# Reordering the first batch's attention front and the u additions of a fused attention and mixer kernel

## The chip, the cores and the metric

The kernel runs on one core of a Trainium2 chip. The metric is the device time of one execution in microseconds. The engines are TensorE (PE, with its weight loads as PEld), VectorE (DVE), ScalarE (ACT), GpSimd (POOL) and SyncE (SP), each with its own queue of instructions that it takes in order; they wait for each other and for transfers through semaphores.

## The reference

Two layers follow each other: a linear attention with a cosine weighting, and a mixer that works first over the tokens and then over the channels.

```
q, k, v: (8, 8, 576, 64) float32     # batch, head, token, head dim
phi(x) = [relu(x) * cos(theta), relu(x) * sin(theta)]      # 128 features, theta = pi/2 * pos / 576
kv  = einsum('bhsf,bhsd->bhfd', phi(k), v);   z = sum over s of phi(k)
x   = einsum('bhsf,bhfd->bhsd', phi(q), kv) / (einsum('bhsf,bhf->bhs', phi(q), z) + 1e-6)
x   = x as (8, 576, 512)
h   = relu(x^T @ w_tok1) @ w_tok2       # w_tok1 576 x 256, w_tok2 256 x 576
u   = x + h^T
out = u + relu(u @ w_ch1) @ w_ch2       # w_ch1 512 x 1536, w_ch2 1536 x 512
```

## The kernel before

The 576 tokens of a batch are four chunks of 128 (ci 0 to 3, R = 4 in the code) and a tail of 64 (ci = R); the tails of two batches share one tile of 128 rows, the even batch in its lower half and the odd batch in its upper half. The chunks' attention outputs are made in the order ORDER = (0, 1, 2, R, 3). All matmuls take bf16 and accumulate in float32 in PSUM.

A batch has a front and a channel part. The front, class Front, consists of:

- feature (L246; k_side and q_side call it twice, for cosine and sine): phi(k) and phi(q) from the loaded float32 tiles kt and qt into kp and qp, on DVE (L263), or on ACT (L261) where on_act is set.
- values (L266): the cast of v into v_aug, whose extra column of ones gives sums. With nc.scalar it is on ACT, with nc.vector on DVE, with nc.gpsimd on POOL.
- ksum, ksum_out and dens, dens_out (L278 to L308): only in batch 0. z is summed by one-column matmuls (ks_ps, L285), copied by ACT (ks_sb, L293), and multiplied with the transposed phi(q) by one-column matmuls (d_ps, L301); DVE adds 1e-6 and takes the reciprocal (L307, L308). In the other batches the column of ones gives the denominator inside num.
- kv and kv_out (L310, L329): kv in two halves of four heads (kv_ps), copied to kv_sb, half 0 by ACT and half 1 by DVE.
- q_trans (L336): phi(q) transposed on PE (qT_ps) and copied by ACT to qpT, L345. From the third batch on a DMA transposes instead.
- num (L354): 65-column matmuls into num_ps and DVE's division into x_sb (L370).
- tok1, tok1_out (L374, L386): x times w_tok1 into two banks b_ps (L383), and the relu into B.
- tok2 (L392): B times w_tok2 (u_ps, L407), DVE's addition of x (u_sb, L410), and, except in batch 0, a cast by ACT.

The channel part, class Channel, first makes h1T in 12 column blocks (c steps: four matmuls into c_ps each, L552, and a relu on ACT, L556), then the outputs in o steps (o_ps, L585; the addition of u on DVE, L590; a DMA out).

The schedule is written by hand: the order in the program is each engine's order. The function first_front (L643) writes out batch 0's front. In it, busy(idle_ps, n) issues n matmuls on zeros (L204) whose result nobody reads. At its end batch 0's u is not yet there in rows: its transposed form is made directly in PSUM, as x turned by the identity (turned_x, L423, 16 matmuls of 128 columns) plus B times w_tok2 (turned_b, L431, 8 matmuls of 512 columns), is copied to uT by ACT and DVE (L712), and feeds the first three c steps (c_block, L562).

From then on the front of the next batch is put between the steps of the channel part of the one before. The method pieces (L462) gives a list of (slot, what, arguments); what stands in slot i is issued behind step i. For the second batch (first is true there) the steps are those of batch 0, of which c steps 3 to 11 come first and o steps from O = 12 on. This list also holds batch 0's own u (before.tok2, in the list as u), POOL's casts of v, and POOL's three loads of w_ch2 (load_w_ch2, L194). The loads of the third batch's k and q wait for the second of those (L765).

PSUM has eight banks: ps_mm has four buffers of one bank, ps_at two buffers of two banks. A new tile in a pool waits until the tile that held its buffer has been read.

Of the kernel before, what the change touches and what calls it, by code (L numbers as in the profile page):

```python
# [9 lines left out]
F32 = mybir.dt.float32  # L10
BF16 = mybir.dt.bfloat16
AF = mybir.ActivationFunctionType
# [4 lines left out]
def kernel(  # L17
# [15 lines left out]
    nc = tc.nc  # L33
# [3 lines left out]
    Dm = H * D  # L37
    S_tok, D_tok = moe_w_tok1.shape
    Dm2, D_ch = moe_w_ch1.shape
    P = 128  # L40
    R = S // P
    SM = R * P
    ST = S - SM
    NSC = R + 1
    NCC = Dm // P
    NT = D_tok // P
    NCH = D_ch // P
    HH = H // 2
    D1 = D + 1
    DP = 80  # L50
    DH = Dm // 2
# [3 lines left out]
    ORDER = (0, 1, 2, R, 3)  # L55
# [16 lines left out]
    ps_mm = ctx.enter_context(tc.tile_pool(name="ps_mm", bufs=4, space=bass.MemoryType.PSUM))  # L72
    ps_at = ctx.enter_context(tc.tile_pool(name="ps_at", bufs=2, space=bass.MemoryType.PSUM))
# [128 lines left out]
    def busy(dst, times):  # L202
        for _i in range(times):
            nc.tensor.matmul(dst, ident, zeros[:, 0:dst.shape[-1]], start=True, stop=True)  # L204

    def cast_tok1(mi):
        nc.scalar.copy(w_tok1[:, :, mi * P:(mi + 1) * P], w_tok1n[:, :, mi * P:(mi + 1) * P])
# [8 lines left out]
    class Front:  # L216
# [109 lines left out]
                                     stop=(ci == NSC - 1 and j == HH - 1),  # L326
                                     skip_group_check=True)

        def kv_out(self, halves=(0, 1)):  # L329
            for g in halves:  # L330
                copy = nc.vector.tensor_copy if g else nc.scalar.copy
                copy(self.kv_sb[g][:, :, 0:D1],  # L332
                     self.kv_ps[g][:, 0:HH * DP]
                     .rearrange("p (j d) -> p j d", d=DP)[:, :, 0:D1])

        def q_trans(self, ci, heads=(0, H), eng=nc.scalar, pool=ps_mm):  # L336
            lo, hi = heads
            qT_ps = pool.tile([P, hi - lo, P], BF16, name="qT_ps",
                              tag="mm" if pool is ps_mm else "at")
            for h in range(lo, hi):  # L340
                nc.tensor.transpose(qT_ps[:, h - lo, :],  # L341
                                    self.q_of(ci)[:, h, :, :].rearrange("p a b -> p (a b)"), ident)
            dst = self.qpT[:, ci * H + lo:ci * H + hi, :] if ci < R else self.tail.qpT[:, lo:hi, :]
            if eng is nc.scalar:
                nc.scalar.copy(dst, qT_ps)  # L345
            else:
                nc.vector.tensor_copy(dst, qT_ps)
# [3 lines left out]
            nc.sync.dma_start_transpose(out=dst,  # L351
                                        in_=self.q_of(ci).rearrange("p h a b -> p (h a b)"))

        def num(self, ci, fill=0, dens=False):  # L354
            num_ps = ps_at.tile([P, 2, 512], F32, name="num_ps", tag="at")
            if fill:
                busy(num_ps[:, 0, HH * DP:512], 1)
            for h in range(H):
                g, j = divmod(h, HH)
                nc.tensor.matmul(num_ps[:, g, j * DP:j * DP + D1], self.qT_of(ci, h),  # L360
                                 self.kv_sb[g][:, j, 0:D1], start=True, stop=True)
            rows = self.rows_of(ci)
            nv = num_ps[rows, :, 0:HH * DP].rearrange("p g (j d) -> p g j d", d=DP)
            if dens:
                den = self.d_sb[ci][rows].rearrange("p (g j) o -> p g j o", g=2)
            else:
                den = small.tile([P, 2, HH, 1], F32, name="den")[rows]
                nc.vector.tensor_scalar_add(den, nv[:, :, :, D:D1], 1e-6)  # L368
                nc.vector.reciprocal(den, den)
            nc.vector.tensor_mul(  # L370
                self.x_of(ci)[rows].rearrange("p (g j d) -> p g j d", g=2, j=HH),
                nv[:, :, :, 0:D], den.to_broadcast([rows.stop - rows.start, 2, HH, D]))
# [10 lines left out]
                nc.tensor.matmul(self.b1_ps[mi], w, self.x_of(ci),  # L383
                                 start=(ci == ORDER[0]), stop=(ci == ORDER[-1]))

        def tok1_out(self, mi, on_act=True):  # L386
            if on_act:
                nc.scalar.activation(self.B1[:, mi, :], self.b1_ps[mi], AF.Relu)  # L388
            else:
                nc.vector.tensor_relu(self.B1[:, mi, :], self.b1_ps[mi])  # L390

        def tok2(self, ci, pool=None, turn=True):  # L392
            res, tail = self.res, self.tail
# [26 lines left out]

            self.res["uT"] = keep.tile([P, R * NCC, P], BF16, name="uT")

        def turned_x(self, dst, kb, first):  # L423

            for ci in range(R):
                nc.tensor.matmul(dst[:, ci * P:(ci + 1) * P],
                                 self.x[:, ci, kb * P:(kb + 1) * P], ident, start=first,
                                 stop=False, skip_group_check=True)
                first = False

        def turned_b(self, dst, kb, cols):  # L431

# [29 lines left out]
        def pieces(self, b, before):  # L462
# [7 lines left out]
            if first:  # L470

                u, act, pool = before.tok2, nc.scalar, nc.gpsimd
                plan = [(4, KS, 0), (4, KS, 1), (5, u, 0, ps_at, False), (5, KS, 2, True),
                        (6, KS, 3, True), (6, u, 1, ps_at, False), (7, KS, R), (7, V, R, nc.vector), (8, V, 0, act),
                        (8, V, 2, pool), (8, load_w_ch2, 0), (8, V, 3, pool),
                        (8, load_w_ch2, 1), (8, load_w_ch2, 2),
                        (8, u, 2, None, False), (9, V, 1, act), (9, u, 3, None, False),
                        (9, QS, 0), (10, u, R, None, False)]
                plan += [(11, KV, ci) for ci in range(NSC)]
                plan += [(11, QS, 1), (11, QS, 2), (11, self.kv_out),  # L480
                         (11, QT, 0, (0, H), act, ps_at), (11, QT, 1), (11, QS, R),
                         (O, QT, 2), (O, N, 0), (O, QS, 3), (O + 1, QT, R),
                         (O + 1, N, 1), (O + 3, N, 2), (O + 3, QT, 3),
                         (O + 5, N, R), (O + 7, N, 3), (O + 8, before.tail_cast)]
            else:
                if late:
                    plan = [(C + 5, V, 1, nc.vector), (C + 5, V, 3, nc.vector),
                            (C + 6, V, 0, nc.scalar), (C + 6, V, 2, nc.scalar),
                            (C + 7, V, R, nc.scalar)]
                else:  # L490
                    plan = [(C + at, V, ci, nc.scalar)
                            for ci, at in enumerate((-1, -1, 0, 1, 2))]

                if odd:
                    sides = ((-4, KS, 0), (-3, QS, 0), (0, KS, 1), (0, KS, 2), (1, QS, 1),
                             (1, KS, 3), (1, QS, 2), (2, QS, 3))
                elif late:
                    sides = ((-4, KS, 0), (-3, KS, 1), (0, KS, 2), (1, KS, 3), (1, QS, 0),
                             (2, QS, 1), (3, QS, 2), (4, QS, 3), (5, KS, R), (9, QS, R))
                else:  # L500
                    sides = ((-4, KS, 0), (-3, KS, 1), (0, KS, 2), (1, KS, 3), (1, QS, 0),
                             (2, KS, R), (2, QS, 1), (3, QS, 2), (4, QS, R), (5, QS, 3))
                for at, side, ci in sides:
                    plan.append((C + at, side, ci))
                    if side == QS:
                        plan.append((C + at, self.q_trans_dma, ci))

                plan += [(C + at, KV, ci) for ci, at in
                         enumerate((7, 7, 8, 8, 8) if late else
                                   (2, 3, 4, 5, 6) if odd else (2, 3, 4, 6, 7))]  # L510
                plan.append((C + (8 if late else 6 if odd else 7), self.kv_out))
# [131 lines left out]
    def first_front(f):  # L643
# [21 lines left out]
            busy(idle_ps, 2)  # L665
            f.ksum(ci)
        f.k_side(R)
        busy(idle_ps, 2)
        f.ksum(R)
        f.values(R, nc.vector)  # L670
        for ci in range(R):
            f.values(ci, nc.scalar, lo_heads)
            f.values(ci, nc.vector, hi_heads)
        f.ksum_out()
        for ci in range(NSC):
            f.kv(ci, (0,))
            if ci < R - 1:
                busy(idle_ps, 1)
        f.kv_out((0,))
        for ci in range(NSC):  # L680
            f.kv(ci, (1,))
        f.kv_out((1,))
        for ci in range(NT):
            cast_tok1(ci)
        permute_tok2(0, nc.scalar.copy)
        permute_tok2(1, nc.gpsimd.tensor_copy)
        f.new_uT()
        t_ps = {}

        dens = f.dens(ORDER[:2])  # L690
        f.dens_out(*dens)
        f.num(ORDER[0], dens=True)
        dens = f.dens(ORDER[2:])
        f.num(ORDER[1], dens=True)
        f.dens_out(*dens)
        for i, ci in enumerate(ORDER):
            if i + 2 < NSC:
                f.num(ORDER[i + 2], dens=True)
            for mi in range(NT):
                f.tok1(mi, (ci,))  # L700
        for mi in range(NT):
            f.tok1_out(mi, on_act=(mi == 0))
        for kb in range(NCC):
            t_ps[kb] = (ps_mm.tile([P, SM], F32, name="t_ps", tag="mm") if kb < 2 else
                        ps_at.tile([P, 2, 512], F32, name="t_ps", tag="at")[:, 0, :])
            f.turned_x(t_ps[kb], kb, first=True)

        c = Channel(0, f.res, f.tail)
        by_block = f.res["uT"].rearrange("p (r k) t -> p r k t", r=R)
# [105 lines left out]
```

## Time and the profile before

| what | us |
|---|---|
| median of 3 runs | 269.42 |
| lowest and highest of them | 268.97, 269.98 |
| the profiled execution | 268.4 |
| its span, first to last instruction | 266.6 |
| PE busy in the span | 260.2 |
| DVE, ACT, POOL busy | 166.1, 127.5, 12.3 |
| batch 0's front, to its first c_block matmul | 24.1 |
| first matmul of batch 0's o steps | 39.0 |

The span begins with the first instruction and ends with the last; the profiled execution's time is 1.8 us longer than its span. Starts in the timelines count from the span's start. A group's length in a timeline reaches to the modelled end of its last instruction, so for matmuls and for DVE instructions the distance from start to start, not the length, tells the rate. PEclk, the granted clock, is 1.00 over the whole span.

### The profile page before, as it was taken

How to read it: one execution, taken by the hardware profiler on the slowest of the kernel's cores; microseconds unless marked ns; L12 is line 12 of the kernel's file. 1: busy time of each engine (PE TensorE's matmuls, PEld its weight loads, DVE VectorE, ACT ScalarE, POOL GpSimd, SP SyncE). 2: the span in 40 equal slices, each digit the busy share in tenths (PEclk: the TensorE clock that was granted, in tenths of full speed). 3: DMA queues.
4: the chain of work that ended last, by engine and by line, in shares of the span. 5: the costliest groups of instructions: out<-in, count | busy, mean ns of one | idle time of the engine just before them, and what ended most of it. 6: DMA issues, size and time to landing. Idle time of an engine off the chain costs nothing.

```text
span 266.6 us, 5133 instructions
## 1 busy us (share of the span) xinstructions
PE 260.2 (98%) x2042; PEld 139.9 (52%) x2063; DVE 166.1 (62%) x381; ACT 127.5 (48%) x224; POOL 12.3 (5%) x26
## 2 busy tenths in 40 slices
PE   7999999999999999999999999999999999999995
PEld 3675466465644455446644455446644455445544
DVE  6974699785665946785565846876565846720022
ACT  4953976428515461646515462546516362516500
POOL 6410130000000000000000000000000000000000
DMA  6999999779998999459984989289974580180022
GB/s 218 331 285 270 331 165 239 277 191 300 172 373 247 293 194 340 111 154 267 178 299 121 294 218 350 65 179 241 242 252 118 157 121 0 50 208 2 2 89 107
DMA packets 91959, 53.68 MB, mean 201 GB/s; under 512 B 59424, under 2 KB 87072, under 8 KB 91936
## 3 DMA queue, kind: packets, MB, share of 16 engines
q1 hardware_dynamic: 88576, 49.62, 70.0%
q0 software_dynamic: 2832, 3.21, 7.3%
q10 hardware_dynamic: 528, 0.52, 0.6%
q8 instruction: 16, 0.26, 0.4%
q14 instruction: 7, 0.06, 0.1%
HBM read 35.85 MB, written 9.44 MB: 170 GB/s over the span
## 4 chain that ended last, share of the span: by engine, by line
PE 86%; DVE 9%; DMA 2%; issue 1%; DVEq 0%
PE o_ps L585 34%; PE c_ps L552 25%; PE b_ps L383 6%; PE u_ps L407 6%; PE ct_ps L572 4%; PE kv_ps L321 3%; PE num_ps L360 3%; DVE x_sb L370 3%; DVE qp L263 2%; DMA qt<-in_q_dram 2%; PE idle_ps L204 1%; PE c_ps L562 1%; DVE u_sb L410 1%; PE qT_ps L341 1%; DVE den L368 1%
## 5 line engine op out<-in xcount | busy, mean ns | idle before, releaser
L585 PE MATMUL o_ps<-w_ch,h1T 128*128 128x512 bf16 (+2 forms) x392 | 92.7, 366 | 0.6
L552 PE MATMUL c_ps<-uT,w_ch 128*128 128x512 bf16 (+2 forms) x384 | 91.9, 372 | 0.1
L556 ACT ACTIVATE h1T<-c_ps 128x512 bf16<-128x512 f32 x93 | 55.4, 598 | 60.0 <-PE c_ps L552 59.7
L585 PEld LDWEIGHTS <-h1T 128*128 128x128 bf16 x408 | 37.6, 98 | 39.4
L552 PEld LDWEIGHTS <-w_ch 128*128 128x128 bf16 x384 | 33.6, 97 | 29.8
L590 DVE TENSOR_TENSOR o_sb<-o_ps,u_sb 128x512 f32<-128x512 f32 (+2 forms) x34 | 22.4, 659 | 29.2 <-PE o_ps L585 27.2
L410 DVE TENSOR_TENSOR u_sb<-u_ps,x_sb 128x512 f32<-128x512 f32 x32 | 21.7, 689 | 5.8 <-PE u_ps L407 5.6
L414 ACT CAST u_bf<-u_sb 128x512 bf16<-128x512 f32 x28 | 17.2, 618 | 16.7 <-DVE u_sb L410 16.7
L407 PE MATMUL u_ps<-B,w_tok 128*128 128x512 bf16 x79 | 22.4, 379 | 0.2
L388 ACT ACTIVATE B<-b_ps 128x512 bf16<-128x512 f32 x8 | 4.8, 597 | 34.1 <-PE b_ps L383 34.1
L370 DVE TENSOR_TENSOR x_sb<-num_ps,den 128x512 bf16<-128x512 f32 x28 | 19.4, 691 | 1.0
L572 PEld LDWEIGHTS <-w_ch 128*128 128x128 bf16 x192 | 13.9, 98 | 8.7
L263 DVE TENSOR_SCALAR kp<-kt,cos_t 128x512 bf16<-128x512 f32 x32 | 15.2, 479 | 4.2 <-DMA kt<-in_k_dram 4.2
L383 PE MATMUL b_ps<-x_sb,w_tok 128*128 128x512 bf16 x63 | 17.7, 379 | 0.1
L572 PE MATMUL ct_ps<-uT_tail,w_ch 128*128 128x128 bf16 x192 | 16.9, 219 | 0.0
L263 DVE TENSOR_SCALAR qp<-qt,cos_t 128x512 bf16<-128x512 f32 (+1 forms) x35 | 15.8, 452 | 0.5 <-DMA qt<-in_q_dram 0.5
L263 DVE TENSOR_SCALAR qp<-qt,sin_t 128x512 bf16<-128x512 f32 (+1 forms) x35 | 15.8, 452 | 0.0
L274 ACT CAST v_aug<-vt 128x512 bf16<-128x512 f32 (+1 forms) x28 | 15.5, 584 | 0.1
L590 DVE TENSOR_TENSOR o_sb<-o_ps,u_tail 128x512 f32<-128x512 f32 x4 | 2.8, 692 | 19.0 <-PE o_ps L585 19.0
L332 DVE CAST kv_sb<-kv_ps 128x260 bf16<-128x260 f32 x8 | 3.4, 431 | 17.1 <-ACT kv_sb L332 15.9
L360 PEld LDWEIGHTS <-qpT 128*128 128x128 bf16 x256 | 11.5, 98 | 4.9 <-issue 0.7
L263 DVE TENSOR_SCALAR kp<-kt,sin_t 128x512 bf16<-128x512 f32 x28 | 13.4, 480 | 0.0
(94 smaller groups left out, 232.1 us busy)
## 6 DMA issues: line engine op xcount, KB each, us to landing
out_dram<-o_sb SPq DMA_DIRECT2D x31, 256.0 KB, 3.2
kt<-in_k_dram SPq DMA_DIRECT2D x7, 1024.0 KB, 6.9
vt<-in_v_dram SPq DMA_DIRECT2D x7, 1024.0 KB, 7.6
qt<-in_q_dram SPq DMA_DIRECT2D x7, 1024.0 KB, 9.1
w_ch<-in_moe_w_ch_dram POOLq DMA_DIRECT2D x4, 384.0 KB, 10.7
w_ch<-in_moe_w_ch_dram POOLq DMA_DIRECT2D x3, 512.0 KB, 8.0
out_dram<-o_sb SPq DMA_DIRECT2D x9, 128.0 KB, 2.3
qtt<-in_q_dram SPq DMA_DIRECT2D x8, 128.0 KB, 5.2
```

Of the source, the lines that this page charges most:

```text
L263: nc.vector.tensor_scalar(o_ap, i_ap, scalar1=w, scalar2=0.0, op0=ALU.mult, op1=ALU.max)
L360: nc.tensor.matmul(num_ps[:, g, j * DP:j * DP + D1], self.qT_of(ci, h), self.kv_sb[g][:, j, 0:D1], start=True, stop=True)
L370: nc.vector.tensor_mul(self.x_of(ci)[rows].rearrange("p (g j d) -> p g j d", g=2, j=HH), nv[:, :, :, 0:D], den.to_broadcast([rows.stop - r ...
L383: nc.tensor.matmul(self.b1_ps[mi], w, self.x_of(ci), start=(ci == ORDER[0]), stop=(ci == ORDER[-1]))
L407: nc.tensor.matmul(u_ps, w_tok2[:, ki, ci * P:(ci + 1) * P], self.B1[:, ki, :], start=(ki == 0), stop=(ki == NT - 1))
L410: nc.vector.tensor_add(u, u_ps[rows], self.x_of(ci)[rows])
L414: nc.scalar.copy(self.ub[:, ci, :], u)
L552: nc.tensor.matmul(c_ps[:, lo:hi], w_ch1[:, ki, mi * P:(mi + 1) * P], uT[:, lo // P:hi // P, ki, :], start=(ki == 0), stop=(ki == NCC - 1))
L556: nc.scalar.activation(self.h1T[:, mi, :], c_ps, AF.Relu)
L572: nc.tensor.matmul(self.ct_ps[:, mi % R, :], w_ch1[:, ki, mi * P:(mi + 1) * P], self.tail.uT[:, ki, :], start=(mi % R == 0 and ki == 0), s ...
L585: nc.tensor.matmul(o_ps, h, w_ch2[:, ki, cols], start=ki == 0, stop=ki == NCH - 1)
L590: nc.vector.tensor_add(o_sb, o_ps, u)
```

## The change

It touches only batch 0's front, the list for the second batch, and one copy.

- In first_front, the four heads' first half of kv is begun ahead of the last ksum, DVE's four casts of v are issued ahead of ACT's, and all denominators (both dens groups with their DVE instructions) come ahead of kv's second half. Of the busy matmuls behind the k features one of two goes for the last ksum, and the three between the kv chunks go.
- kv's second half is copied by ACT instead of DVE, between the two casts of w_tok1.
- Two of the four turned_x groups do their first three chunks ahead of the last tok1 pair.
- B's relu is done in two halves of 256 columns on each of ACT and DVE.
- In the second batch's list, batch 0's u(0) to u(3) move to c steps 3 to 6, with PSUM from ps_at, and the first k features to step 6, behind u(3); u(R) moves from step 10 to step 8. The sine of q chunk 2 moves from DVE to ACT.
- The copy of the transposed tail of an odd batch's q, where PE transposes it, takes only that batch's 64 columns.

```
@@ Front.kv_out, q_trans, tok1_out, turned_x
-        def kv_out(self, halves=(0, 1)):
+        def kv_out(self, halves=(0, 1), on_act=(0,)):
             for g in halves:
-                copy = nc.vector.tensor_copy if g else nc.scalar.copy
+                copy = nc.scalar.copy if g in on_act else nc.vector.tensor_copy
...
+            if ci == R and self.rows.start:
+                dst, qT_ps = dst[:, :, self.rows], qT_ps[:, :, self.rows]
...
+        def tok1_out(self, mi, on_act=True, cols=slice(0, Dm)):
...
-        def turned_x(self, dst, kb, first):
-            for ci in range(R):
+        def turned_x(self, dst, kb, chunks=range(R)):
+            for ci in chunks:
@@ Front.pieces, first
-                plan = [(4, KS, 0), (4, KS, 1), (5, u, 0, ps_at, False), (5, KS, 2, True),
-                        (6, KS, 3, True), (6, u, 1, ps_at, False), (7, KS, R), (7, V, R, nc.vector), (8, V, 0, act),
+                plan = [(3, u, 0, ps_at, False), (4, u, 1, ps_at, False), (5, u, 2, ps_at, False),
+                        (6, u, 3, ps_at, False), (6, KS, 0), (6, KS, 1), (6, KS, 2, True),
+                        (7, KS, 3, True), (8, u, R, None, False), (8, KS, R),
+                        (8, V, R, nc.vector), (8, V, 0, act),
                         (8, V, 2, pool), (8, load_w_ch2, 0), (8, V, 3, pool),
-                        (8, load_w_ch2, 1), (8, load_w_ch2, 2),
-                        (8, u, 2, None, False), (9, V, 1, act), (9, u, 3, None, False),
-                        (9, QS, 0), (10, u, R, None, False)]
+                        (8, load_w_ch2, 1), (8, load_w_ch2, 2), (9, V, 1, act), (9, QS, 0)]
                 plan += [(11, KV, ci) for ci in range(NSC)]
-                plan += [(11, QS, 1), (11, QS, 2), (11, self.kv_out),
+                plan += [(11, QS, 1), (11, QS, 2, True), (11, self.kv_out),
@@ first_front
         f.k_side(R)
-        busy(idle_ps, 2)
-        f.ksum(R)
         f.values(R, nc.vector)
         for ci in range(R):
+            f.values(ci, nc.vector, hi_heads)
+        for ci in range(R - 1):
             f.values(ci, nc.scalar, lo_heads)
-            f.values(ci, nc.vector, hi_heads)
+        f.kv(0, (0,))
+        busy(idle_ps, 1)
+        f.ksum(R)
         f.ksum_out()
-        for ci in range(NSC):
-            f.kv(ci, (0,))
-            if ci < R - 1:
-                busy(idle_ps, 1)
+        f.values(R - 1, nc.scalar, lo_heads)
+        f.kv(1, (0,))
+        f.kv(2, (0,))
+        dens = f.dens(ORDER[:2])
+        f.dens_out(*dens)
+        f.kv(3, (0,))
+        f.kv(R, (0,))
         f.kv_out((0,))
+        cast_tok1(0)
+        dens = f.dens(ORDER[2:])
+        f.dens_out(*dens)
         for ci in range(NSC):
             f.kv(ci, (1,))
-        f.kv_out((1,))
-        for ci in range(NT):
-            cast_tok1(ci)
+        f.kv_out((1,), on_act=(1,))
+        cast_tok1(1)
+        f.num(ORDER[0], dens=True)
+        f.num(ORDER[1], dens=True)
...
-        dens = f.dens(ORDER[:2])
-        f.dens_out(*dens)
-        f.num(ORDER[0], dens=True)
-        dens = f.dens(ORDER[2:])
-        f.num(ORDER[1], dens=True)
-        f.dens_out(*dens)
...
+            if ci == R:
+                for kb in range(2):
+                    t_ps[kb] = ps_mm.tile([P, SM], F32, name="t_ps", tag="mm")
+                    f.turned_x(t_ps[kb], kb, range(R - 1))
-        for mi in range(NT):
-            f.tok1_out(mi, on_act=(mi == 0))
+        for cols in (slice(0, DH), slice(DH, Dm)):
+            for mi in range(NT):
+                f.tok1_out(mi, on_act=(mi == 0), cols=cols)
         for kb in range(NCC):
-            t_ps[kb] = (ps_mm.tile([P, SM], F32, name="t_ps", tag="mm") if kb < 2 else
-                        ps_at.tile([P, 2, 512], F32, name="t_ps", tag="at")[:, 0, :])
-            f.turned_x(t_ps[kb], kb, first=True)
+            if kb < 2:
+                f.turned_x(t_ps[kb], kb, (R - 1,))
+                continue
+            t_ps[kb] = ps_at.tile([P, 2, 512], F32, name="t_ps", tag="at")[:, 0, :]
+            f.turned_x(t_ps[kb], kb)
```

More of the change, by code (lines that the diff above doesn't have):

```diff
@@ L352, in q_trans_dma, with num @@
                                         in_=self.q_of(ci).rearrange("p h a b -> p (h a b)"))
-        def num(self, ci, fill=0, dens=False):
+        def num(self, ci, dens=False):
             num_ps = ps_at.tile([P, 2, 512], F32, name="num_ps", tag="at")
-            if fill:
-                busy(num_ps[:, 0, HH * DP:512], 1)
             for h in range(H):
@@ L384, in tok1 @@
                                  start=(ci == ORDER[0]), stop=(ci == ORDER[-1]))
-        def tok1_out(self, mi, on_act=True):
+        def tok1_out(self, mi, on_act=True, cols=slice(0, Dm)):
             if on_act:
-                nc.scalar.activation(self.B1[:, mi, :], self.b1_ps[mi], AF.Relu)
+                nc.scalar.activation(self.B1[:, mi, cols], self.b1_ps[mi][:, cols], AF.Relu)
             else:
-                nc.vector.tensor_relu(self.B1[:, mi, :], self.b1_ps[mi])
+                nc.vector.tensor_relu(self.B1[:, mi, cols], self.b1_ps[mi][:, cols])
         def tok2(self, ci, pool=None, turn=True):
@@ L421, in new_uT @@
             self.res["uT"] = keep.tile([P, R * NCC, P], BF16, name="uT")
-        def turned_x(self, dst, kb, first):
-            for ci in range(R):
+        def turned_x(self, dst, kb, chunks=range(R)):
+            for ci in chunks:
                 nc.tensor.matmul(dst[:, ci * P:(ci + 1) * P],
-                                 self.x[:, ci, kb * P:(kb + 1) * P], ident, start=first,
+                                 self.x[:, ci, kb * P:(kb + 1) * P], ident, start=(ci == 0),
                                  stop=False, skip_group_check=True)
-                first = False
         def turned_b(self, dst, kb, cols):
```

## The prediction

> **What bounds the kernel now.** I read the page first, then the timelines of PE, DVE, ACT and POOL up to 48 us, then the chain of waits and the landings of the loads that the second batch needs. The page's first part:
>
> ```profile
> PE 260.2 (98%) x2042; PEld 139.9 (52%) x2063; DVE 166.1 (62%) x381; ACT 127.5 (48%) x224; POOL 12.3 (5%) x26
> ```
>
> PE is busy for 98% of the span, so an edit pays only where it takes PE work or a PE wait away, and it costs wherever it makes PE wait. Some of that PE work is filler (idle_ps, L204). The timeline of PE for the stage of the change (start, length, group):
>
> ```profile
> 1.38 5.00 PE L204 MATMUL idle_ps<-zeros,ident 128*128 128x512 bf16 x12 [1.38 <-POOL ident masks.py:199]
> ...
> 15.00 0.38 PE L204 MATMUL idle_ps<-zeros,ident 128*128 128x512 bf16 x1
> ...
> 18.41 0.38 PE L383 MATMUL b_ps<-x_sb,w_tok 128*128 128x512 bf16 x1
> ...
> 21.49 1.05 PE L426 MATMUL t_ps<-ident,x_sb 128*128 128x128 bf16 x16
> 22.38 1.89 PE L434 MATMUL t_ps<-w_tok,B 128*128 128x512 bf16 x8
> 24.11 2.75 PE L562 MATMUL c_ps<-uT,w_ch 128*128 128x512 bf16 x12
> 26.70 2.75 PE L552 MATMUL c_ps<-uT,w_ch 128*128 128x512 bf16 x12
> ```
>
> By starts, a 512-column matmul takes 0.216 us (2.59/12), a 128-column one 0.056 (0.89/16), a 65-column one 0.030, a one-column one 0.025. From 26.7 us the second batch's front is woven into PE's c steps, and DVE feeds it. DVE and POOL in their timelines, then the chain that ended last:
>
> ```profile
> 28.76 0.48 DVE L263 TENSOR_SCALAR kp<-kt,cos_t 128x512 bf16<-128x512 f32 x1 [3.75 <-DMA kt<-in_k_dram]
> ...
> 32.44 0.83 DVE L263 TENSOR_SCALAR kp_tail<-ktt,cos_t 64x512 bf16<-64x512 f32 x1
> 33.20 0.83 DVE L263 TENSOR_SCALAR kp_tail<-ktt,sin_t 64x512 bf16<-64x512 f32 x1
> 33.95 0.82 DVE L276 CAST v_aug<-vtt 64x512 bf16<-64x512 f32 x1
> 34.80 1.29 DVE L410 TENSOR_TENSOR u_sb<-u_ps,x_sb 128x512 f32<-128x512 f32 x2
> ```
>
> ```profile
> 32.38 0.62 POOL L276 CAST v_aug<-vt 128x512 bf16<-128x512 f32 x1 [11.74 <-DMA vt<-in_v_dram]
> 32.94 0.77 POOL L196 DMA_DIRECT2D w_ch<-in_moe_w_ch_dram  x1
> 33.70 0.79 POOL L276 CAST v_aug<-vt 128x512 bf16<-128x512 f32 x1
> 34.44 1.49 POOL L196 DMA_DIRECT2D w_ch<-in_moe_w_ch_dram  x2
> ```
>
> ```profile
> 37.47 1.24 DVE qp L263 x4
> 38.72 0.26 issue
> 38.98 0.43 DVE kv_sb L332
> 39.41 0.59 PE qT_ps L341 x8
> 40.00 0.24 PE num_ps L360 x8
> ```
>
> DVE runs without a pause from 28.76, when the second batch's kt lands, to kv_sb at 38.98, and PE takes the queries' transposes right behind it. DVE has no slack here, so work moved ahead of its features is the first thing to price.
>
> **First batch, up to turned_b.** (1) Four fillers go: 4 x 0.216 = 0.86 off PE. (2) All 40 denominator matmuls now stand ahead of kv's second half: 40 x 0.025 = 1.0, neither new nor dropped. Following PE with these durations from ksum(3), which ends at 13.57: kv(0) 13.57, filler 13.69, ksum(R) 13.91 to 14.11, kv(1) and kv(2) to 14.34. ACT writes ks_sb, done 14.45, so the first 16 denominators wait 0.16 and run 14.50 to 14.90. kv's first half ends 15.14, the other 24 denominators 15.74, kv's second half 16.33 (before: 16.06). (3) kv_sb's second half goes to ACT, behind one cast: 16.53 to 16.91 (on DVE before: 16.26 to 16.69). The first x starts at 17.28 against 17.21. (4) DVE's second pair of denominator instructions, which stood between x(1) and x(2) and held x(2) to 19.13, is done by then, so x(2) starts at 18.48 and x(3) at 19.81 (before: 20.34). PE is then full: its b_ps and num groups run to 20.44, six early turned_x to 20.78, the last b_ps pair to 21.21, the other ten turned_x to 21.77. So turned_b starts at 21.77, not 22.38: **0.61 us gained**. (5) B's relu in halves: DVE's first half ends at about 21.83, just ahead of the second turned_b matmul at 21.98. Whole it would end at 22.1 and cost 0.15; before it was hidden by turned_x.
>
> **Second batch.** (6) The u adds, 0.60 each by starts, now stand ahead of all kp features on DVE. PE does c(3), u(0), c(4), u(1), c(5), u(2), c(6), u(3): four times 0.864 + 0.432 from 26.09 (26.70 less 0.61), so u(3) leaves PE at 31.27 and DVE at 32.07. DVE is idle between these adds, and the first kp starts at 32.07 though kt landed at 28.76. From there to kv_sb: six kp instructions at 0.395 (2.37), u(R) 0.60, two kp_tail 0.80, v 0.41, five qp 1.97, in all 6.15 at the undisturbed rate. Three of DVE's rows beside POOL's casts took 0.76, 0.75 and 0.85 by starts instead of 0.40: 1.14 in excess. POOL waits for vt's landing as before, so I keep 1.14; none of it, or twice it, are the bounds, and I take the equal value because the same two casts meet the same kind of instruction. kv_sb then starts at 39.36 (before: 38.98). qT(1) needs the second qp pair, ready at 39.10, and starts there instead of 38.5. Behind it come two o_ps (0.43), qT(2) (0.45), and num(0) at 40.43 against 39.84: **0.59 us late**. PE waits some 1.5 us before that, at kv's tail, qT(0) and qT(1), and gives back the 0.61 and 0.59 more. (7) One qp sine moves to ACT (0.81 there, L261): ACT has 0.91 and 0.63 idle before kv_sb, so it hides; uncovered it would cost 0.8. (8) The last qT copied by half saves ACT about 0.45 of a 1.04 copy; 0.52 of idle follows it, so it gives nothing. (9) u's PSUM now comes from the pool of two double banks; each add is done 1 us before its bank is wanted, and a 0.22 gap of PE at 35.33 goes, which the DVE wait eats. After num(0) PE has no gap in which to win 0.59 back, so it stays to the end.
>
> **The sum.** Span 266.6 + 0.6 = 267.2; with the 1.8 around it (268.4 - 266.6) 269.0. The profiled execution lies 1.0 under the median of the runs, 269.42, so I forecast 270.0.
>
> **What the loads allow.** PE may not start o_ps before w_ch2 lands. The answer on the three loads of L196, and SP's timeline where it waits for the second of them:
>
> ```profile
> DMA to landing us min/median/max: 5.9/8.0/9.8
> ```
>
> ```profile
> 42.58 0.38 SPq L86 DMA_DIRECT2D kt<-in_k_dram  x1
> ```
>
> Issued at 32.94, 34.44 and 35.19, taken in order, the thirds land at about 38.8, 42.4 and 45.0 (the load at 42.58 waits for the second). PE reached o_ps at 38.96, and the second third at 42.78. So whatever the first batch gains, at most 0.1 to 0.3 survives this gate, and POOL's queue, which feeds it, is not changed.
>
> **Rivals.** *DVE is not the late one*: if POOL cost DVE nothing, the second qp pair would be ready at 37.96, PE would meet the w_ch2 gate and be 0.1 to 0.3 ahead: 269.2. Against it stand the three slow rows. Chance 0.08.
>
> *w_ch2 and DVE suffer from each other (slower).* POOL's second and third issue at 34.44 to 35.93 lay beside u adds at their usual 0.60; now kp and v instructions lie there. If these slow as beside the casts, four of them become two and 0.76 more is lost: 271 at least. If the issues give way instead, the landing decides: PE reaches the second third at 43.4, one us after its landing now, and each us beyond is paid whole; pushed behind the last qp at 39.3, it would land at 47.3 and cost 3.9. For it: three slowed rows, the second of them mostly beside an issue. Against it: the four w_ch1 issues at 10.55 lay beside kp features of 0.40, unslowed, and took 0.79 to 0.84 against 0.75. Chance 0.24. [...]
>
> *The clock falls (slower).* The last filler ends at 15.21 and the next 512-column matmul starts at 18.41: 3.2 us of small work, after which b_ps still ran at 0.216. Now it is 13.91 to 18.25, 4.3 us. The first 12 fillers took 4.83, 0.40 each; at that rate as many matmuls behind 18.25 would cost 12 x 0.184 = 2.2, and as DVE's late start hangs on PE's u(3) it adds whole: 272.2. It decides if PE's b_ps pairs stand 0.43 a matmul apart. For it: the longer stretch. Against: 3.2 us did nothing. Chance 0.12. [...]
>
> **How the numbers follow.** The forecast's own case has 0.51, from 269.2 (no excess on DVE) to 270.9 (0.9 more). The bound of 0.5%, 1.35 us, is about what a measurement of this kernel can tell from no change. The forecast and the first rival lie within it but for 0.02: same 0.57. The two slower rivals and that 0.02 lie beyond: slower 0.38. I find no way to a gain over 1.35, as fillers, stalls and the gate leave 0.3; 0.05 is kept for a step misread. Range 268.9 to 272.2: the runs' scatter below the gate's best, and the clock's price above.
>
> **What would show it.** Right: turned_b near 21.8; four u adds on DVE before the first kp, which starts near 32 with idle ahead of it; PE waits at qT; num(0) of the second batch near 40.4. Wrong: kp at 28.8, the slow DVE rows gone or many more, b_ps at 0.43 spacing, o_ps waiting for w_ch2, or a changed time per batch after 50 us.

## The result and the profile after

| | before | changed |
|---|---|---|
| median of 22 executions, us | 269.27 | 270.15 |
| profiled execution, its span | 268.4, 266.6 | 269.59, 267.8 |
| turned_b begins | 22.38 | 21.89 |
| first kp of the second batch on DVE | 28.76 | 32.20 |
| second half of its kv_sb, DVE | 38.98 | 39.86 |
| its num(0) begins | 39.84 | 40.94 |

The time is 1.0031 times that of the kernel before, 95% interval 1.0018 to 1.0044: 0.8 us slower (0.5 to 1.2), within the 1.35 us that the forecast counts as no change, and clear of zero. One execution of each kernel was slow (343.70 us, and 342.49 us at a granted clock of 0.755) and is left out of the ratio, and the trace figures above and the lines below are from a profile of the changed kernel at a clock of 1.00, run as e1_after.

PE in its timeline (start, length, group, and in brackets the idle time before it and what ended it):

```profile
21.89 1.89 PE L433 MATMUL t_ps<-w_tok,B 128*128 128x512 bf16 x8
...
36.63 1.02 PE L551 MATMUL c_ps<-uT,w_ch 128*128 128x512 bf16 x4 [1.20 <-DVE u_tail L410]
37.49 1.14 PE L321 MATMUL kv_ps<-v_aug,kp 128*128 128x65 bf16 x32
...
38.81 0.62 PE L341 MATMUL qT_ps<-ident,qp 128*128 128x128 bf16 x8
39.60 0.62 PE L341 MATMUL qT_ps<-ident,qp 128*128 128x128 bf16 x8 [0.17 <-DVE qp L263]
40.06 0.59 PE L584 MATMUL o_ps<-w_ch,h1T 128*128 128x512 bf16 x2
```

DVE in its timeline:

```profile
30.30 0.69 DVE L410 TENSOR_TENSOR u_sb<-u_ps,x_sb 128x512 f32<-128x512 f32 x1 [0.60 <-PE u_ps L407]
31.59 0.69 DVE L410 TENSOR_TENSOR u_sb<-u_ps,x_sb 128x512 f32<-128x512 f32 x1 [0.60 <-PE u_ps L407]
32.20 0.74 DVE L263 TENSOR_SCALAR kp<-kt,cos_t 128x512 bf16<-128x512 f32 x1
32.86 0.82 DVE L263 TENSOR_SCALAR kp<-kt,sin_t 128x512 bf16<-128x512 f32 x1
33.61 0.82 DVE L263 TENSOR_SCALAR kp<-kt,cos_t 128x512 bf16<-128x512 f32 x1
34.35 0.72 DVE L263 TENSOR_SCALAR kp<-kt,sin_t 128x512 bf16<-128x512 f32 x1
35.00 0.99 DVE L263 TENSOR_SCALAR kp<-kt,cos_t 128x512 bf16<-128x512 f32 x2
```

And the chain that ended last, in order of time:

```profile
31.59 0.69 DVE u_sb L410
32.28 1.50 DVE kp L263 x3
33.79 0.57 issue
34.35 1.64 DVE kp L263 x3
35.99 0.59 DVE u_tail L410
36.58 0.03 issue
36.61 0.89 DVE kp_tail L263 x2
37.50 0.34 DVE v_aug L276
37.84 0.03 issue
37.87 1.68 DVE qp L263 x4
39.56 0.05 issue
39.60 0.62 PE qT_ps L341 x8
```

The front is 0.49 us ahead at turned_b, though DVE's first qp began 0.14 later in this execution (5.53 against 5.39): counted from there it gained 0.63. Not all of that is the edit's. The fourth ksum, ahead of which nothing was changed, began at 13.43 against 13.37, so 0.08 of it lies ahead of the edits (in the trace before DVE waited 0.43 for the first batch's kt, here it did not), and from that ksum on the gain is 0.55. Then DVE has the path without a break from u(3) at 31.59 to the transposes at 39.60: it waits 0.60 between the u additions for PE, starts kp 3.4 us later than before, and PE, which has come early, stands 1.20 at c(11). At the first addition of an output (DVE, L589) the kernel is 1.07 us behind the one before, from the third addition on 1.18, and this is the difference of the spans' last outputs too (264.62 against 263.45).

### The profile page after: what moved, and what is told of

Same layout as the page of the kernel before. It is cut to its first block, busy times and chain, and to the rows that moved or that the text cites. A ratio compares the mean times of both kernels' runs of the same rounds, so it can differ in the third digit from the quotient of the medians.

```text
span 340.7 us, 5150 instructions
## 1 busy us (share of the span) xinstructions
PE 335.0 (98%) x2059; PEld 163.6 (48%) x2059; DVE 164.7 (48%) x380; ACT 130.1 (38%) x227; POOL 15.6 (5%) x26
## 4 chain that ended last, share of the span: by engine, by line
PE 97%; DMA 1%; DVE 0%; ACT 0%; issue 0%; DVEq 0%
PE o_ps L584 36%; PE c_ps L551 31%; PE u_ps L407 7%; PE b_ps L383 7%; PE ct_ps L571 4%; PE num_ps L360 3%; PE kv_ps L321 3%; PE qT_ps L341 2%; PE idle_ps L204 2%; DMA qt<-in_q_dram 1%; PE c_ps L561 1%; PE t_ps L433 1%; PE t_ps L426 0%; PE d_ps L301 0%; PE ks_ps L285 0%; DVE x_sb L370 0%
## 5 line engine op out<-in xcount | busy, mean ns | idle before, releaser
L584 PE MATMUL o_ps<-w_ch,h1T 128*128 128x512 bf16 (+2 forms) x408 | 121.0, 445 | 0.0
L551 PE MATMUL c_ps<-uT,w_ch 128*128 128x512 bf16 (+2 forms) x384 | 117.3, 452 | 0.0
L584 PEld LDWEIGHTS <-h1T 128*128 128x128 bf16 x408 | 42.8, 111 | 57.1 <-issue 56.8
L551 PEld LDWEIGHTS <-w_ch 128*128 128x128 bf16 x384 | 39.1, 112 | 42.4 <-issue 41.6
L589 DVE TENSOR_TENSOR o_sb<-o_ps,u_sb 128x512 f32<-128x512 f32 (+2 forms) x34 | 22.4, 659 | 50.0 <-PE o_ps L584 49.9
L407 PE MATMUL u_ps<-B,w_tok 128*128 128x512 bf16 x80 | 28.2, 459 | 0.0
L388 ACT ACTIVATE B<-b_ps 128x512 bf16<-128x512 f32 (+1 forms) x9 | 4.8, 549 | 48.3 <-PE b_ps L383 48.3
L571 PEld LDWEIGHTS <-w_ch 128*128 128x128 bf16 x192 | 16.8, 111 | 12.7 <-issue 12.6
L383 PE MATMUL b_ps<-x_sb,w_tok 128*128 128x512 bf16 x64 | 22.6, 462 | 0.0
L368 DVE TENSOR_SCALAR den<-num_ps 128x8 f32<-128x8 f32 (+1 forms) x35 | 5.8, 166 | 24.1 <-PE num_ps L360 24.1
L360 PE MATMUL num_ps<-kv_sb,qpT 128*128 128x65 bf16 x256 | 15.2, 208 | 0.8 <-DVE x_sb L370 0.5
L589 DVE TENSOR_TENSOR o_sb<-o_ps,u_tail 128x512 f32<-128x512 f32 x4 | 2.8, 692 | 27.1 <-PE o_ps L584 27.1
L407 PEld LDWEIGHTS <-w_tok 128*128 128x128 bf16 x80 | 9.3, 116 | 13.7 <-issue 13.7
```

Source lines behind the costliest of these rows:

```text
L383: nc.tensor.matmul(self.b1_ps[mi], w, self.x_of(ci), start=(ci == ORDER[0]), stop=(ci == ORDER[-1]))
L407: nc.tensor.matmul(u_ps, w_tok2[:, ki, ci * P:(ci + 1) * P], self.B1[:, ki, :], start=(ki == 0), stop=(ki == NT - 1))
L551: nc.tensor.matmul(c_ps[:, lo:hi], w_ch1[:, ki, mi * P:(mi + 1) * P], uT[:, lo // P:hi // P, ki, :], start=(ki == 0), stop=(ki == NCC - 1))
L571: nc.tensor.matmul(self.ct_ps[:, mi % R, :], w_ch1[:, ki, mi * P:(mi + 1) * P], self.tail.uT[:, ki, :], start=(mi % R == 0 and ki == 0), s ...
L584: nc.tensor.matmul(o_ps, h, w_ch2[:, ki, cols], start=ki == 0, stop=ki == NCH - 1)
L589: nc.vector.tensor_add(o_sb, o_ps, u)
```

## The experiments

Ratios are to executions of the kernel before on the same chip. Its medians there were 269.17 us for e1 to e4 (26 executions), 269.01 for e5 to e8 (29) and 269.01 for e9 to e12 (30). Single traces start up to 0.7 us apart (DVE's first qp from 5.39 to 6.11, by the landing of the first q), so between traces I also use the distance from turned_b to num(0): 17.46 in the kernel before.

**e1_after**: the changed kernel again.

> The changed kernel itself, for its trace. Theory (DVE is the late one): about 0.6 us over the kernel before; turned_b starts near 21.8 (22.38 before), the first kp on DVE near 32.1 with DVE idle between the four u additions, three kp or v instructions slowed to 0.76 to 0.85 beside POOL's casts, kv_sb by DVE near 39.4, num(0) of the second batch near 40.4 (39.84 before). Rival (w_ch2 against DVE): more than three slow DVE instructions between 32 and 37, or the second third of w_ch2 landing after 43.4 with o_ps waiting for it. Rival (clock): b_ps pairs 0.43 a matmul apart near 18 to 20, turned_b later than before.

269.97 against 269.17, ratio 1.0041 (1.0023 to 1.0060). The theory's marks came where they were put, the last two 0.5 us later than put. The six kp took 3.71 us (32.20 to 35.91) where 2.37 is undisturbed: 1.34 of excess, 1.22 of it on four instructions and not three. The thirds of w_ch2, issued from 32.60 on, had 5.9, 7.7 and 10.1 us to landing against 5.9, 8.0 and 9.8, and o_ps waited for none.

**e2_front**: the changed front, the old list.

```
-  plan = [(3, u, 0, ps_at, False), ... (6, KS, 0), ...]      # the changed list
+  plan = [(4, KS, 0), (4, KS, 1), (5, u, 0, ps_at, False), ...]   # as before
-  (11, QS, 2, True)
+  (11, QS, 2)
```

> The change in batch 0's front alone (denominators, kv_sb, turned_x, relu in halves, copy of half a qT); the second batch's list is as before. Theory: turned_b 0.6 us earlier than before, but DVE still begins kp when kt lands at 28.76 and the first third of w_ch2 still lands near 38.8, so only 0.1 to 0.3 us of it is kept: 0.1 to 0.3 us under the kernel before. Rival (the front's gain would be whole if u stayed): 0.6 us under. Rival (clock, or the front itself is slower): 0 to 2 us over.

269.06, ratio 0.9998 (0.9983 to 1.0013). The rival, 0.6 us kept, lies outside this interval; the 0.1 to 0.3 of the theory can't be told from nothing. **e3_list** is the counterpart: the old front, the changed list.

> The changed list for the second batch alone (u additions sooner, one qp sine on ACT); the front is as before. Theory: u(3) leaves PE 0.6 us later than in the changed kernel, the first kp starts near 32.7, num(0) near 41.0: 1.2 us over the kernel before (39.84 plus 1.2). Rival (w_ch2 against DVE): the cost comes at o_ps behind the landing of w_ch2, not at qT, and is then the same with the early or the late front, 0.6 to 0.8 us over. Rival (the list costs nothing, the front costs): 0.

270.20, ratio 1.0054 (1.0033 to 1.0075). The list costs 0.9 to 2.0 us, and the front alone is worth 0.5 either way at most. That the cost is smaller with both (1.18 at the last output in e1's trace, 1.38 in e3's) is not shown by the times, whose intervals overlap. From turned_b to num(0) it is 18.56 in e3 and 19.05 in e1: a front that ends sooner buys a longer wait. Part of it is POOL's: its first cast of v starts at 32.02 in e3 and 32.05 in e1, where the landing of vt puts it, and takes 0.62, so DVE's kp, from 32.96 on in e3 and from 32.20 on in e1, miss it in e3 and meet it in e1; the six took 3.22 and 3.71.

**e4_mixed**: two u additions fill DVE's wait for kt, the other three go behind features again.

```
-  (5, u, 2, ps_at, False), (6, u, 3, ps_at, False), (6, KS, 0), (6, KS, 1), (6, KS, 2, True),
-  (7, KS, 3, True), (8, u, R, None, False), (8, KS, R), (8, V, R, nc.vector), ...
+  (5, KS, 0), (5, KS, 1), (5, KS, 2, True), (6, KS, 3, True), (6, u, 2, ps_at, False),
+  (7, KS, R), (7, V, R, nc.vector), (7, u, 3, ps_at, False), ... (9, u, R, None, False), ...
```

> The changed kernel with u(0) and u(1) ahead of the kp features as there, but u(2), u(3) and u(R) put back between and behind the features (steps 6, 7 and 9), so that DVE meets kt soon after it lands. Theory: first kp near 29.5, kv_sb by DVE near 38.0, PE no longer waits at qT and meets the w_ch2 gate at 38.8 instead: 0.1 to 0.3 us under the kernel before, some 0.8 us under the changed kernel. Rival (w_ch2 against DVE): no better than the changed kernel, since kp instructions still lie beside POOL's issues. Rival (clock): no better either, as the front is the changed one.

268.97, ratio 0.9996 (0.9979 to 1.0013): the loss of 1.1 us in e1 is gone, by the place of the u additions alone. kp starts at 29.95 and kv_sb is at 38.42. What ends last now, in the timelines of PE of e4 and of e2:

```profile
39.20 0.61 PE L585 MATMUL o_ps<-w_ch,h1T 128*128 128x512 bf16 x2 [0.43 <-DMA w_ch<-in_moe_w_ch_dram]
```

```profile
72.77 0.42 PE L360 MATMUL num_ps<-kv_sb,qpT_tail 128*128 128x65 bf16 x8 [0.26 <-DMA qpT_tail<-qp_tail]
```

e4 meets the w_ch2 gate. e2 did not (w_ch2 had landed), was 0.40 ahead of the kernel before up to 56 us, and lost all of it by 80 us at the third batch's transposed q tail, whose load stands on SP behind another transposition: the matmuls ahead of that wait began at 71.91 against 72.31, those behind it at 72.77 against 72.74. That second gate I had not seen.

**e8_bank**: is it c(11)'s wait for u(R)'s bank that costs?

```
-  (8, u, R, None, False)
+  (8, u, R, ps_at, False)
```

> The changed kernel with u(R)'s PSUM from the pool of two double banks, so that c(11) need not wait for DVE's u(R) addition, for which PE stood 1.20 us. Theory (DVE's queue is what ends last): PE starts kv 1.2 us earlier and then stands as long at kv's tail and at qT, num(0) stays within 0.1 us and the time within 0.2 us of the changed kernel. Rival (the bank of u(R) is the cost): 1.0 to 1.2 us faster than the changed kernel, level with the kernel before.

270.57, ratio 1.0049 (1.0033 to 1.0066): nothing comes back. PE's timeline:

```profile
38.15 0.40 PE L321 MATMUL kv_ps<-v_aug,kp_tail 128*128 128x65 bf16 x8 [0.46 <-DVE v_aug L276]
39.07 0.62 PE L341 MATMUL qT_ps<-ident,qp 128*128 128x128 bf16 x8 [0.51 <-DVE qp L263]
39.86 0.62 PE L341 MATMUL qT_ps<-ident,qp 128*128 128x128 bf16 x8 [0.17 <-DVE qp L263]
```

The wait at c(11) is gone and turns up at kv's tail and at both transposes, as DVE delivers them: 1.14 in place of 1.20 and 0.17. From turned_b to num(0) it is 18.89 against e1's 19.05. The bank only chose where PE stood.

**e5_casts**: what do POOL's casts cost DVE?

```
-  (8, V, 2, pool), (8, load_w_ch2, 0), (8, V, 3, pool),
+  (8, load_w_ch2, 0), (10, V, 2, act), (11, V, 3, act),     # load 0 made to wait for vt
```

> The changed kernel with POOL's two casts of v given to ACT (steps 10 and 11), the first w_ch2 load held on vt's landing by a dependency instead. It takes away what slows DVE's kp instructions. Theory (DVE late by the order, 7.66 us from the first kp to kv_sb, 1.3 of it beside POOL's casts): kp at 0.40 each again, kv_sb by DVE near 38.5, num(0) of the second batch 1.1 to 1.3 us earlier than in the changed kernel, that is 0.0 to 0.2 us under the kernel before in time. Rival (POOL's load issues slow DVE as well): the kp instructions beside the three issues stay at 0.65 to 0.75, and half or less of the 1.3 us comes back: 0.4 to 0.7 over the kernel before. Rival (the bank of u(R) is the cost): no more than 0.3 us comes back.

269.37, ratio 1.0015 (0.9997 to 1.0032): 0.4 us over the kernel before where the changed kernel has 0.8 to 1.1, so 0.4 to 0.7 came back, not clear of noise, as the intervals overlap. That is the time which the rival on POOL's issues put here, and not the theory's 0.0 to 0.2. DVE in its timeline:

```profile
32.79 0.48 DVE L265 TENSOR_SCALAR kp<-kt,cos_t 128x512 bf16<-128x512 f32 x1
33.18 0.62 DVE L265 TENSOR_SCALAR kp<-kt,sin_t 128x512 bf16<-128x512 f32 x1
33.72 0.47 DVE L265 TENSOR_SCALAR kp<-kt,cos_t 128x512 bf16<-128x512 f32 x1
34.11 0.61 DVE L265 TENSOR_SCALAR kp<-kt,sin_t 128x512 bf16<-128x512 f32 x1
34.64 0.99 DVE L265 TENSOR_SCALAR kp<-kt,cos_t 128x512 bf16<-128x512 f32 x2
```

The six kp took 2.76 us (32.79 to 35.55), so 0.95 of the 1.34 excess was the casts'. With the three issues still beside them (32.70 to 35.40) two kp took 0.54 and 0.53 by starts, not the 0.65 to 0.75 of the rival, and the last two 0.91 together for 0.79, so the issues cost DVE something, 0.39 in all. What else was won on DVE did not reach the end, as kv now waited for ACT's cast:

```profile
38.49 0.40 PE L323 MATMUL kv_ps<-v_aug,kp 128*128 128x65 bf16 x8 [0.46 <-ACT v_aug L276]
```

**e6_front_qtt** and **e7_best** load the third batch's q tails sooner on SP:

```
   if b == 0 and i == NCH + 13:
       load_batch(2, "v")
-      load_batch(2, "k", main=False)
-  if b == 1 and i == 1:
-      load_batch(2, "q", main=False)
+      load_batch(2, "kq", main=False)
```

> The front alone (list as before), and the third batch's q tails loaded with its k tails, one c step of the second batch and some 6 us sooner. The front alone was 0.40 us ahead of the kernel before until 56 us in the trace and lost it at the transposed q tail of the third batch, which landed at 72.7. Theory (that landing is a second gate that nothing in the change moves): the wait there goes and 0.3 to 0.5 us under the kernel before is kept to the end. Rival (the 0.4 was a matter of that one profile): no difference, 0.0 to 0.1.

> All that the readings point to: the changed front, u(0) and u(1) ahead of the kp features and the other u behind them, POOL's casts of v on ACT with the w_ch2 loads issued as soon as vt lands, the third batch's q tails loaded earlier. Theory: neither DVE, nor w_ch2, nor the q tail makes PE wait; what is left is PE's own work, 0.6 us less in the front and 0.2 less at the banks of u: 0.5 to 0.8 us under the kernel before, 1.3 to 1.9 under the changed one. Rival (another gate follows): 0.0 to 0.3 under the kernel before.

Neither theory held: 269.09, ratio 1.0013 (0.9994 to 1.0033), which is the rival's no difference, and 269.57, ratio 1.0018 (1.0007 to 1.0028), slower than the kernel before. In both traces the two loads hold up what stands behind them on SP, and PE waits 0.70 and 0.94 for a transposed q chunk at the third batch's num(0). e7 also kept e5's casts on ACT, with 0.60 of waiting at kv. Neither is a better kernel, and no clean price of the second gate came from them.

e6's trace showed something else. By stretches of its span (columns: span; busy us and instructions of PE, PEld, DVE, ACT, POOL; granted clock; DMA share; GB/s):

```profile
16.00:18.00 2.00, 1.51 (x46) 1.32 (x43) 0.83 (x3) 1.48 (x4) 0.00 (x0) 1.00 1.11 265
18.00:20.00 2.00, 1.38 (x16) 1.05 (x17) 1.63 (x3) 0.00 (x0) 0.00 (x0) 0.61 1.16 215
20.00:22.00 2.00, 2.00 (x18) 1.11 (x16) 1.07 (x2) 1.32 (x2) 1.34 (x2) 0.54 1.17 212
```

The clock fell some 4 us behind the last filler, to 0.61 and 0.54 in the mean of these stretches, and turned_b came 17.99 us behind DVE's first qp and not 16.36 as in e1. So I counted executions whose mean clock is under 0.995: 13 of 95 among the kernels with the changed front (the changed one and e1, e2, e4 to e8), none of 85 of the kernel before. In the changed kernel's first 21 they are four, at 270.59 in the mean against 269.93 of the others. The others still lie 0.7 above the kernel before (269.22 in the mean of 21), so the clock is not the loss.

**e9_fill** and **e10_nofill** ask whether the fillers do it.

```
# e9: e4, and                                   # e10: the changed kernel, but
+  idle2 = ps_mm.tile([P, Dm], F32, ...)        -  busy(idle_ps, 1)      # ahead of ksum(R)
+  busy(idle2, 2)                               -  busy(idle_ps, 2)      # ahead of ksum(3)
   f.num(ORDER[0], dens=True)
   f.num(ORDER[1], dens=True)
+  busy(idle2, 2)
```

> The mixed list (u(0) and u(1) ahead of the kp features, the others behind) with four fillers of 512 columns put back where PE waits anyway: two ahead of num(0), two behind num(1). The granted clock fell below 0.995 in 13 of 95 executions of kernels with the changed front, and in none of 62 with the old one. Theory (the changed front lets the clock fall at times, the fillers hold it): no execution below 0.995, PE's starts unchanged but for at most 0.1 us, and 0.1 to 0.4 us under the kernel before. Rival (the fall has nothing to do with the fillers): one or two executions of twelve below 0.995, as in the mixed list without fillers, and level with the kernel before.

> The changed kernel without its last three fillers: the two ahead of the fourth ksum and the one ahead of the last. Theory (small matmuls and waits let the clock fall): the stretch without a 512-column matmul grows from 4.3 to some 5 us and the clock falls below 0.995 in a third of the executions or more; those cost 0.7 to 1.7 us, the others are level with the changed kernel. Rival (the fall is random): again about one in seven.

e10: all 7 executions under 0.995; 270.31, ratio 1.0051 (1.0032 to 1.0069). e9: none of 12; 268.78, ratio 1.0007 (0.9986 to 1.0027). e10's stretches:

```profile
16.00:18.00 2.00, 1.47 (x34) 1.26 (x31) 1.01 (x3) 1.15 (x3) 0.00 (x0) 0.71 1.15 230
18.00:20.00 2.00, 1.84 (x19) 1.29 (x19) 1.39 (x3) 1.21 (x2) 1.10 (x2) 0.50 1.16 209
```

So taking fillers out makes the clock fall, every time in e10. That four put in elsewhere hold it is likely and not more: if 13 in 95 fall, none in the 24 of e9 and e12 would still come about by chance in some 3 of 100 cases. The price was less than expected: e10 lies 0.34 above e1's 269.97, measured on another occasion. Its trace shows where the rest went. turned_b came 17.25 us behind the first qp, 0.89 later than in e1, but POOL's casts, at 31.37 and 32.69, now ran beside u additions. The six kp took 2.65 (33.22 to 35.87) in place of 3.71, and num(0) came 35.23 behind the first qp against 35.41 in e1. The gain expected of e9 did not show; in its trace w_ch2 landed late and o_ps waited 1.1 us for it.

**e11_before_nofill**: the kernel before without the four fillers, and nothing else.

```
-  busy(idle_ps, 2)          # ahead of ksum(R)
+  busy(idle_ps, 1)
...
-  if ci < R - 1:            # between the chunks of kv's first half
-      busy(idle_ps, 1)
```

> The kernel before without the same four fillers that the change removes, and nothing else. Theory: kv's second half ends 0.65 us sooner and turned_b starts about 0.6 us sooner, of which no more than 0.1 to 0.3 us is kept, since kt, w_ch2 and the third batch's q tail set the pace later; the stretch without a 512-column matmul grows from 3.2 to about 4 us, and the clock falls in some executions. Rival (the denominators' new place is what gained the 0.6): turned_b is no more than 0.2 us sooner.

268.93, ratio 1.0004 (0.9986 to 1.0022). turned_b came 16.50 us behind the first qp, 0.49 sooner than before (16.99) where e1 has 0.63, and counted from the fourth ksum 0.42 sooner where e1 has 0.55: most of the front's gain is the fillers'. One of 12 executions was under 0.995. The time did not move: in its trace o_ps waited 1.1 us for w_ch2.

**e12_gates**: e9, the first w_ch2 load ahead of POOL's casts and the q tails loaded by POOL.

```
-  (8, V, 2, pool), (8, load_w_ch2, 0), (8, V, 3, pool),
+  (8, load_w_ch2, 0), (8, V, 2, pool), (8, V, 3, pool),     # load 0 made to wait for vt
   if b == 1 and i == 1:
-      load_batch(2, "q", main=False)
+      ... load_tail(io_tails[1][0], q, g, nc.gpsimd) for g in (2, 3), behind w_ch2
```

> The mixed list with the four fillers, and both gates opened: the first w_ch2 load issued by POOL as soon as vt has landed, ahead of its two casts, and the third batch's q tails loaded by POOL behind w_ch2 instead of by SP behind a transposition. Theory: PE waits for neither, num(0) 0.5 us and the end 0.4 to 0.7 us under the kernel before. Rival (a further gate follows): 0.0 to 0.2 under.

268.43 against 269.01, ratio 0.9990 (0.9976 to 1.0005), no execution of 12 under 0.995. That is 0.3 us under the kernel before, between the theory's 0.4 to 0.7 and the rival's 0.2. PE no longer waited at the q tail, but still 0.5 us at w_ch2. Its ratio lies 0.4 to 0.5% below the changed kernel's (1.0031, and 1.0041 in e1), and the intervals do not meet; against the kernel before it is not shown to be faster.

## Why the prediction was right, point by point

- The front, steps 1 to 5: 0.61 us gained was forecast; in e1 it was 0.55 from the fourth ksum on and 0.63 from the first qp (16.36 against 16.99), turned_b at 21.89 against a forecast 21.77. So near a hit is partly luck: in other traces with the changed front and the clock up, the gain from the fourth ksum on was 0.28 (e4), 0.29 (e8), 0.48 (e2), 0.54 (e7) and 0.55 (e5). e11 gives 0.42 to 0.49 of it to the fillers. That the halves of the relu save 0.15 was not measured by itself.
- The u additions, step 6: the first kp at 32.07 was forecast, 32.20 measured. DVE's stretch to kv_sb was 7.66 and not 7.29. POOL's excess was 1.34 on the kp for 1.14, u(R) took 0.70 for 0.60 (the u addition ahead of a kp_tail took 0.70 in the trace before too, 31.74 to 32.44), and the v cast and the qp 0.07 more than put. With the start 0.13 late that makes kv_sb 0.50 late, and num(0) came at 40.94 and not 40.43. With POOL's casts gone, in e5, the six kp took 2.76 for 3.71, 0.95 us less. e3 and e4 show that this order is the loss; the excess by itself is not, since the kernel before has 1.14 of it too.
- Step 7, a qp sine on ACT hides: ACT was done with it and kv_sb's first half at 39.30, ahead of PE's num(0). But the cover was thin: two more casts on ACT in e5 made ACT the late one. Step 8, the half copy: its row is 0.59 for 1.04, with 1.21 of ACT's idle time ahead of its next copy, so nothing was to be had.
- Step 9 was wrong in one part: u(R)'s bank was not free 1 us ahead, c(11) waited 1.20 for it. e8 shows that it costs nothing, because DVE is later still. PE waited 1.37 in all for some 1.5 forecast, at c(11) and qT(1) and not at kv's tail.
- What the loads allow: the w_ch2 gate is there (0.43 in e4, 1.1 in e9 and e11, 0.5 in e12), but moves by a us and more from trace to trace (its first third landed at about 38.3 in e2 and 40.0 in e9), and it is not the only one: the 0.40 of e2 passed it and was lost at the third batch's q tail. The reason given for the cap was half of it.
- Rivals: w_ch2 did not land later: its three loads had 5.9, 7.7 and 10.1 us to landing in e1 against 5.9, 8.0 and 9.8 before. The other half of that rival was there in small: more than three slow rows, of which POOL's issues have 0.39 at most, below the rival's 0.76 to 3.9. The clock rival, priced 2.2 us with a chance of 0.12, is real in 13 of 95 executions, at 0.7 us in the changed kernel and not 2.2. Its price was too high for two reasons: by the estimate below the half clock lasted only some 3.4 us, of which at most half, 1.7, can be lost, and in e10 DVE's kp, come later, met less of POOL's casts (2.65 for the six against 3.71). PE waited for at most 0.54 at once ahead of the fall in e6, and 0.35 in e10, and the clock fell all the same. That the small matmuls, and not the waits between them, let it fall is how I read it; no run tells the two apart.
- The sum, 0.6 us, stands against 0.8 (0.5 to 1.2) over many executions: the mechanism is the one given, and DVE's stretch is what was short. In single traces the miss is wider: num(0) 1.10 late for 0.59, the spans 1.2 apart for 0.6. The median of 270.15 lies so near the forecast 270.0 by luck: the 1.0 that was added because the profiled execution lay under the median is 0.56 for the changed kernel's trace, which makes up for most of the 0.6 by which the sum in the traces was short.

## What to carry to other kernels

Before work is moved ahead on an in-order engine, ask when its input is ready: an addition that waits for another engine holds up features whose data have landed long ago. A gain in an early stage counts only if the loads behind it are not the next thing to be waited for, so try the two halves of a change apart. Fillers that look like waste may be what holds TensorE's clock (with three fewer than in the changed kernel it was under 0.995 in 7 of 7 executions, for 13 of 95); try them where it waits anyway, and read the granted clock of many executions, not of one trace.

## What had not been expected of the hardware

The clock fell with no wait of PE over 0.54 us in the stretch ahead of it. In e10, where 5.6 us (12.94 to 18.57) hold only matmuls of 1 and 65 columns and waits of up to 0.35 us, it was 0.50 between 18 and 20 us in the trace and under 0.995 on the mean in 7 of 7 executions. With one filler more than that and two ahead of the fourth ksum, so that the stretch is 4.4 us in e1, it was so in 13 of 95; at 3.7 us (e11) in one of 12; at 3.2 us (the kernel before) in none of 85; and with four more fillers where PE waits, in none of 24 (e9 and e12). An estimate from the granted clock of 2 us stretches (0.71, 0.50 and 0.93 from 16 us on in e10, 0.61 and 0.54 from 18 us on in e6), taken as one step down to 0.50 and one up: it was down from 16.84 to 20.28 us in e10 and from 18.44 to 21.84 in e6, about 3.4 us both times, beginning about 4 us behind the last filler. Half the clock for 3.4 us takes 0.006 off the mean of a span of 268, so by this estimate one such fall makes the mean of 0.994 that the profiled executions of e6 and e10 have. At the start of the span the row of the granted clock reads 1.00, while the first ten fillers of the kernel before stood 0.42 apart (1.38 to 5.62), as two b_ps matmuls did in e6 with the clock down (20.09 to 20.93); why the row does not show it there is not known.

And it is not beside POOL's casts alone that a DVE tensor_scalar took longer. Beside POOL's issues of w_ch2, with no cast of POOL's near, two kp took 0.54 and 0.53 in e5 against 0.395, and a kp_tail 0.64 against 0.40 in e7. It is not always so: beside POOL's four w_ch1 issues, at 10.55 to 13.76 in the kernel before, the kp took their 0.40, and what makes the difference is not shown.
